# U = v_m w made for four f tiles in one run, and the second matmul's halves reordered at a group's end

## The chip, the cores and the metric

The kernel runs on one core of a Trainium2 chip. The metric is the device time of one execution in microseconds (us). The core has a matrix engine (PE, with its weight loads shown apart as PEld), a vector engine (DVE), a scalar engine (ACT), GpSimd (POOL) and SyncE (SP, which here only issues DMAs).

## The reference, cut to what matters

```python
# batch 8, heads 8, seq 576, head_dim 64, n_mem 32
a   = softmax(phi, axis=seq)
k_m = einsum('bhsm,bhsd->bhmd', a, k);  v_m = einsum('bhsm,bhsd->bhmd', a, v)
attn = softmax(q @ k_m.T / 8, axis=mem)
x   = (attn @ v_m) laid out as (8*576, 512)
gate = sigmoid(x @ w_gate);  val = x @ w_val          # 512 -> 1536
out = (gate * val) @ w_out                            # 1536 -> 512
```

## The kernel before, in words

The kernel never forms x. Since x @ w = attn @ (v_m w), it makes U = v_m w for each batch b and each *f tile* (128 of the 1536 columns of w_gate and the same 128 of w_val, `NFT` = 12 tiles), and multiplies attn by U. Every float32 product is made of three matmuls on halves called hi and lo (hi·hi, hi·lo, lo·hi).

**One step** (b, f) of the main loop (L911) has two halves of the 576 rows, c = 0 (256 rows) and c = 1 (320 rows, of which 64 are put aside in `left` and multiplied later by `out_left`). A half is:
- `gate_of`: 12 matmuls `pu_t<-at_..,u_..` on PE. c = 0 uses one PSUM bank for gate and value, c = 1 uses two. The pool `pu` has `NB` = 4 banks, given out in turn.
- `gate_sig` (ACT, sigmoid, L135), `gate_mul` (DVE, product, L636), `gate_hi` (ACT, cast, L647), `gate_lo` (DVE, difference, L150).
- later `out_half`: 6 matmuls `acc<-wo_..,g_..` with w_out, into the four other PSUM banks (`acc`). Halves wait in the list `pend`; one is taken out whenever it holds `LAG` = 3.

**U** is made for a pair of f tiles (`make_u`, L547). `u_banks` issues 8 matmuls `pu_t<-wg,vT`, one for each head, each on a 64x32 tile of the array and 512 columns wide, into two PSUM banks. `u_hi` (ACT, two casts, L567) and `u_lo` (DVE, two differences, L150) then bring them to SBUF in `u_tiles`, of which the pool keeps two. The heads 4 to 7 read the second half (k = 1) of the weights of an f tile, the heads 0 to 3 the first half (k = 0). The main loop makes the next pair's U in every second step, between its two halves.

**The order of steps.** The steps come in groups of `TURN` = 4 f tiles: for f 0-3 the batches 0 to 3 in turn, then f 4-7 for the same batches, then f 8-11 (these batches are added up through rows that are written to and read back from DRAM, `part`, with `row` as the buffer, `out_end`, L687), and then the batches 4 to 7 with all 12 f tiles each. The first 8 steps are part of a list written out by hand (`OPENING`), which also makes U for the batches 0 and 1 and for (2, f 0-1); the main loop begins with step 8 (`DONE`).

**Work beside it.** The weights come as 64-bit words and are turned into float32 on the way: a job (f, k) is a load on the POOL queue, a magnitude on ACT (L236) and four operations on DVE (L241, L242, L245, L248); k = 0 and 1 are the two halves of w_gate and w_val, k = 2 is w_out, which has a cast (`wo_hi`, L278) and a difference (`wo_lo`) more. `CONVERT` says at which step each job is issued. The attention of the following batch (scores, maximum, exponent, `normalize`, `turn`, and the sums of k and v, `remember`) is spread over the steps in pieces (`sides`); where the next step is another batch's, what is left of the pieces is issued before U is made.

The program order of PE is the order of the Python calls. On ACT and DVE a scheduler orders the work, within chains that keep the gate's sigmoids, products and differences ahead of the weight jobs.

Of the kernel before, what the change touches and what calls it, by code (L numbers as in the profile page):

```python
# [18 lines left out]
B, H, S, D, M = 8, 8, 576, 64, 32  # L19
# [17 lines left out]
TURN = 4  # L37
DONE = 8
# [2 lines left out]

FIRST = 4
CONVERT = {
# [4 lines left out]
}  # L48
# [29 lines left out]
def attn_moe_kernel(  # L78
# [24 lines left out]
    def bank():  # L103
        name = next(turn_of) if spread else None
        if name is None:
            return pu.tile([P, 512], F32, name="pu_t")
        return po.tile([P, 512], F32, name=name)
# [40 lines left out]
    def rest(lo, x, hi):  # L148

        return nc.vector.tensor_tensor(lo, x, hi.bitcast(F32), op=ALU.subtract)  # L150
# [11 lines left out]
    def matmul(*args, **kw):  # L162
        in_turn(nc.tensor.matmul, *args, **kw)
# [145 lines left out]
    def load_q(b, cuts=(0, 1)):  # L309
        if (b, "q") not in loaded:  # L310
            loaded[b, "q"] = att([P, NKT * S], "q")
        for c in cuts:
            for u, n in PIECES[c]:
                o = u * NKT * 2 * P
                move(loaded[b, "q"][:, o : o + NKT * n], qT[b][:, o : o + NKT * n])
# [117 lines left out]
    def of_head(b, w, p):  # L433

        rs = slice((p % 2) * D, (p % 2 + 1) * D)
        hs = slice((p % 4) * M, (p % 4 + 1) * M)
        return rs, kvTs[b][w][rs, p // 4, hs]
# [101 lines left out]
    def again(b):  # L539
        new_at(b)  # L540
        for d, a in zip(kept[b], at[b]):
            move(a.rearrange("p r n -> p (r n)").bitcast(F32), d)
# [1 line left out]

    U = {}

    def make_u(b, fs):  # L547
        u_banks(b, fs)
        u_hi(b, fs)
        u_lo(b, fs)  # L550

    def u_banks(b, fs):

        nf = len(fs)
        pb = [bank()[:, : nf * 256].rearrange("p (f x) -> p f x", f=nf) for _ in range(2)]
        for p in range(H):
            rs, l = of_head(b, 1, p)
            js = slice((p // 2) * M, (p // 2 + 1) * M)
            r = wg[rs, fs[0] : fs[0] + nf, ORDER[b % 2][p] // 2, :]
            matmul(pb[p % 2][js], l, r, start=True, stop=True)  # L560
        loaded[b, "u", fs[0]] = pb

    def u_hi(b, fs):
        pb, nf = loaded[b, "u", fs[0]], len(fs)
        U[b, fs[0]] = u_tiles()
        for r in range(2):
            nc.scalar.copy(U[b, fs[0]][0][:, r, :nf], pb[r])  # L567

    def u_lo(b, fs):
        pb, nf = loaded.pop((b, "u", fs[0])), len(fs)  # L570
        hi, lo = U[b, fs[0]]
        for r in range(2):
            last_u[0] = rest(lo[:, r, :nf], pb[r], hi[:, r, :nf])
        for i, f in enumerate(fs):
            U[b, f] = (hi[:, :, i], lo[:, :, i])
# [22 lines left out]
    def gate_half(b, f, c):  # L598
        gate_of(b, f, c)
        gate_sig(b, f, c)  # L600
        gate_mul(b, f, c)
        gate_hi(b, f, c)
        gate_lo(b, f, c)
# [56 lines left out]
    def out_half(b, f, c, at_start, at_end):  # L660
        out_of(b, f, c, at_start, at_end)
        if at_end:
            out_end(b, f, c)
        if (b, f + 1) in ends and c:
            for t in range(2):
                rows[b, t] = row_of(b, t)

    def out_of(b, f, c, at_start, at_end):
        hi, lo = G.pop((b, f, c))
        w_hi, w_lo = wo_of(f)  # L670
        for j in range(2):
            t = 2 * c + j
            if at_start:
                acc[b, t] = po.tile([P, DM], F32, name=f"acc{t}")
            ts = slice(j * P, (j + 1) * P)
            o = acc[b, t]
            matmul(o, hi[:, ts], w_hi, start=at_start, stop=False)
            matmul(o, hi[:, ts], w_lo, start=False, stop=False)
            matmul(o, lo[:, ts], w_hi, start=False, stop=at_end)

    def out_end(b, f, c, js=range(2)):
        for j in js:
            t = 2 * c + j
            o = acc.pop((b, t))
            st = rows.pop((b, t), None) or row_of(b, t)
            if (b, t) in part:
                nc.vector.tensor_tensor(st, o, st, op=ALU.add)  # L687
                part.pop((b, t))
            elif t % 2:
                nc.scalar.copy(st, o)  # L690
            else:
                nc.vector.tensor_copy(st, o)
            if f == NFT - 1:
                move(out[b * S + t * P : b * S + (t + 1) * P, :], st)
            else:
                part[b, t] = dram.tile([P, DM], F32, name=f"part{b}_{t}_{f}")
                move(part[b, t], st)
# [3 lines left out]
    def row_of(b, t):  # L701

        st = mb.tile([P, DM], F32, name="row", bufs=2)
        if (b, t) in part:
            move(st, part[b, t], "rows")
        return st

    def u_tiles():
        return [mb.tile([P, 2, 2, 256], F32R, name=f"u_{p}", bufs=2) for p in ("hi", "lo")]
# [3 lines left out]
    def out_left(pair, f0, nf):  # L713

        hi, lo = [t.rearrange("p r f x -> p (r f x)").rearrange("p (f x) -> p f x", x=P) for t in u_tiles()]
        for k in range(0, nf, TURN):
            raw = left.pop((pair, (f0 + k) // TURN))
            nc.scalar.copy(hi[:, k : k + TURN], raw)
            rest(lo[:, k : k + TURN], raw, hi[:, k : k + TURN])
        yield  # L720
        o = bank()
        for k in range(nf):
            w_hi, w_lo = wo_of(f0 + k)
            matmul(o, hi[:, k], w_hi, start=(k == 0), stop=False)
            matmul(o, hi[:, k], w_lo, start=False, stop=False)
            matmul(o, lo[:, k], w_hi, start=False, stop=(k == nf - 1))
        if f0 == 0:
            left_sum[pair] = mb.tile([P, DM], F32, name="wo_raw")
            nc.vector.tensor_copy(left_sum[pair], o)
        else:  # L730
            st = left_sum.pop(pair)
            nc.vector.tensor_tensor(st, o, st, op=ALU.add)
            for j in range(2):
                b = 2 * pair + j
                move(out[b * S + SF * P : (b + 1) * S, :], st[j * TAIL : (j + 1) * TAIL, :])
        yield


    def run(*parts):
        for p in parts:  # L740
            for _ in p:
                pass
# [39 lines left out]
    steps = [(b, f, f == f0, f == f1 - 1) for b, f0, f1 in turns for f in range(f0, f1)]  # L782
    ends = {(b, f) for b, f, _, at_end in steps if at_end}
    begin = {(b, f): i for i, (b, f, at_start, _) in enumerate(steps) if at_start}

    u_at = {}
    for i, (b, f, _, _) in enumerate(steps):
        if f % 2 == 0:
            u_at[i - 1] = (b, [f, f + 1])

    spare = ident.bitcast(mybir.dt.bfloat16)
    idle = po.tile([P, 512], F32, name=f"acc{SF - 1}")
# [104 lines left out]
        begin[turns[k - 1][:2]]: b for k, (b, f0, _) in enumerate(turns) if b < QUAD and f0  # L897
    }
    lefts = {begin[2, NFT - TURN]: 0, begin[QUAD, 0]: 1, begin[QUAD + 2, 0]: 2}
    lefts = {i + 2 * k: (p, 8 * k, 8 - 4 * k) for i, p in lefts.items() for k in range(2)}  # L900
    lefts[begin[B - 1, 0] + 8] = (B // 2 - 1, 0, 8)

    beside, slots = iter(()), iter(())

# [5 lines left out]
    pend = [(1, f, c, False, f == 3) for f in (2, 3) for c in range(2)][-LAG:]  # L910
    for i, (b, f, at_start, at_end) in enumerate(steps):  # L911
        if i < DONE:
            continue
        if i in sides:
            run(beside)
            beside, slots = chain(*sides[i][1:]), iter(sides[i][0])
        if i in returns:
            again(returns[i])
        if i > max(CONVERT) and (QUAD, "q") not in loaded:
            load_q(QUAD)  # L920
        extra = out_left(*lefts[i]) if i in lefts else iter(())
        gate_half(b, f, 0)
        for job in CONVERT.get(i, ()):
            with behind():
                convert(*job)
        next(extra, None)
        if i in u_at:
            if steps[i + 1][0] != b:
                run(beside)
            make_u(*u_at[i])  # L930
        while len(pend) >= LAG:
            out_half(*pend.pop(0))
        pend.append((b, f, 0, at_start, at_end))
        go_on()
        gate_half(b, f, 1)
        while len(pend) >= LAG:
            out_half(*pend.pop(0))
        pend.append((b, f, 1, at_start, at_end))
        next(extra, None)
        go_on()  # L940
        del U[b, f]
# [58 lines left out]
```

## Time and profile before

| | |
|---|---|
| median of 3 runs | 763.07 us (761.05 to 764.59) |
| the profiled execution | 762.09 us |
| its span in the profile | 760.3 us |
| PE busy | 737.1 us (97%) |
| DVE busy | 434.6 us (57%) |
| ACT busy | 337.6 us (44%) |
| granted TensorE clock | 0.992 of full speed |

The profiled execution's time is 1.8 us more than its span, which begins and ends with the first and last thing that the profile shows. A row of the timeline gives the start, the duration, the engine, the line, the operation, output<-inputs, shapes and a count; a matmul's duration overlaps the next one's, so the pace of PE is read from start to start. In square brackets stands idle time of the engine ahead of the row and what ended it.

### The profile page before, as it was taken

What the parts mean: (1) busy time and instruction counts of PE and PEld (TensorE: products, weight loads), DVE (VectorE), ACT (ScalarE), POOL (GpSimd) and SP (SyncE); (2) the same over time, 40 slices, a digit from 0 to 9 for tenths busy, and PEclk for the clock granted to TensorE, in tenths of its full rate; (3) what the DMA queues carried; (4) which work ended last, traced back from release to release, by engine and by line L of the source; (5) the groups of instructions that cost most, each with busy time, mean ns of one, the idle gap of its engine ahead of it and who ended that gap; (6) DMA issues with size and microseconds to landing.
All of it is one profiled execution on the core that took longest, in us unless ns stands there. A gap on an engine that the chain in (4) does not pass through costs nothing.

```text
span 760.3 us, 13810 instructions
## 1 busy us (share of the span) xinstructions
PE 737.1 (97%) x5651; PEld 610.0 (80%) x5651; DVE 434.6 (57%) x824; ACT 337.6 (44%) x784; POOL 14.1 (2%) x30
## 2 busy tenths in 40 slices
PE   7998999998999999999999999999999999999997
PEld 5676887786887888888887888887887888888886
DVE  7897748995777754456646533365333743343422
ACT  4387545575443443235442643355333533333322
POOL 0000000011000000000000000000000000000000
PEclk9899999999999999999999999999999999999999
DMA  9977255767555453432462240011000000010002
GB/s 358 363 287 288 84 208 186 263 227 244 213 196 187 170 181 112 159 113 75 132 212 70 91 152 6 1 56 63 2 2 28 28 15 1 1 56 1 1 1 69
DMA packets 30655, 93.17 MB, mean 123 GB/s; under 512 B 3456, under 2 KB 4480, under 8 KB 28032
## 3 DMA queue, kind: packets, MB, share of 16 engines
q1 hardware_dynamic: 22528, 71.31, 25.8%
q0 software_dynamic: 3456, 12.58, 5.0%
q10 hardware_dynamic: 4608, 8.39, 3.5%
q8 instruction: 44, 0.72, 0.4%
q14 instruction: 19, 0.16, 0.1%
HBM read 69.73 MB, written 22.54 MB: 121 GB/s over the span
## 4 chain that ended last, share of the span: by engine, by line
PE 86%; ACT 4%; DVE 4%; DMA 3%; issue 1%; SPq 0%; DVEq 0%; ACTq 0%
PE pu_t L160 51%; PE acc L160 35%; DMA kvm<-in_kvm_dram 2%; ACT L135 2%; ACT ph L135 1%; DMA part<-row 1%; DVE q L513 1%; ACT sg L135 0%; DMA row<-part 0%; DVE u_lo L150 0%; DVE sg L636 0%; DVE e L492 0%; DVE g_lo L150 0%; SPq L146 0%; DVE at_lo L150 0%
## 5 line engine op out<-in xcount | busy, mean ns | idle before, releaser
L160 PE MATMUL pu_t<-at_hi,u_hi 128*128 128x256 f32 (+1 forms) x760 | 227.0, 299 | 0.9 <-DVE sg L636 0.9
L160 PE MATMUL pu_t<-at_hi,u_lo 128*128 128x256 f32 (+1 forms) x760 | 223.0, 293 | 1.1 <-DVE u_lo L150 1.1
L160 PE MATMUL pu_t<-at_lo,u_hi 128*128 128x256 f32 (+1 forms) x760 | 223.4, 294 | 0.0
L636 DVE TENSOR_TENSOR sg<-pu_t,sg 128x256 f32<-128x256 f32 (+1 forms) x190 | 86.4, 455 | 190.0 <-ACT sg L135 117.3
L135 ACT ACTIVATE sg<-pu_t 128x256 f32<-128x256 f32 (+1 forms) x190 | 78.3, 412 | 209.5 <-PE pu_t L160 196.0
L160 PE MATMUL acc<-wo_hi,g_hi 128*128 128x512 f32 x384 | 156.9, 409 | 1.4 <-DVE row L687 1.4
L160 PEld LDWEIGHTS pu_t<-at_hi,u_hi 128*128 128x128 f32 x760 | 142.7, 188 | 12.3 <-DVE sg L636 2.2
L160 PE MATMUL acc<-wo_hi,g_lo 128*128 128x512 f32 x384 | 151.3, 394 | 0.0
L160 PE MATMUL acc<-wo_lo,g_hi 128*128 128x512 f32 x384 | 151.1, 394 | 0.0
L160 PEld LDWEIGHTS pu_t<-at_lo,u_hi 128*128 128x128 f32 x760 | 142.7, 188 | 6.5
L160 PEld LDWEIGHTS pu_t<-at_hi,u_lo 128*128 128x128 f32 x760 | 142.5, 187 | 1.5 <-DVE u_lo L150 1.5
L647 ACT CAST g_hi<-sg 128x256 fp32r<-128x256 f32 x192 | 78.0, 406 | 131.7 <-DVE sg L636 118.3
L150 DVE TENSOR_TENSOR g_lo<-sg,g_hi 128x256 fp32r<-128x256 f32 x192 | 80.6, 421 | 56.0 <-ACT g_hi L647 55.8
L160 PEld LDWEIGHTS acc<-wo_hi,g_hi 128*128 128x128 f32 x384 | 72.2, 188 | 49.7 <-issue 38.5
L160 PEld LDWEIGHTS acc<-wo_hi,g_lo 128*128 128x128 f32 x384 | 72.4, 189 | 17.1
L160 PEld LDWEIGHTS acc<-wo_lo,g_hi 128*128 128x128 f32 x384 | 72.4, 189 | 8.7
L150 DVE TENSOR_TENSOR u_lo<-pu_t,u_hi 128x512 fp32r<-128x512 f32 x93 | 60.6, 684 | 3.8 <-ACT u_hi L567 2.6
L160 PE MATMUL pu_t<-wg,vT 64*32 64x512 f32 x744 | 52.8, 601 | 2.8 <-DVE wg L248 2.8
L567 ACT CAST u_hi<-pu_t 128x512 fp32r<-128x512 f32 x93 | 49.9, 587 | 5.3 <-PE pu_t L160 3.6
L687 DVE TENSOR_TENSOR row<-acc,row 128x512 f32<-128x512 f32 x32 | 21.9, 687 | 8.7 <-DMA row<-part 5.1
L135 ACT ACT_TABLE_LOAD x20 | 25.7, 1283 | 2.1 <-DVE g_lo L150 1.0
L160 PE MATMUL acc<-ident 128*128 128x256 bf16 x155 | 23.0, 313 | 1.4 <-POOL ident masks.py:199 1.4
(110 smaller groups left out, 574.1 us busy)
## 6 DMA issues: line engine op xcount, KB each, us to landing
kvm<-in_kvm_dram SPq DMA_DIRECT2D x16, 1024.0 KB, 8.2
q<-in_qT_dram SPq DMA_DIRECT2D x16, 512.0 KB, 5.3
part<-row SPq DMA_DIRECT2D x32, 256.0 KB, 2.3
row<-part ACTq DMA_DIRECT2D x32, 256.0 KB, 3.1
out_dram<-row SPq DMA_DIRECT2D x32, 256.0 KB, 2.0
words<-in_wgv_dram POOLq DMA_DIRECT2D x10, 512.0 KB, 4.8
ph<-in_phiT_dram SPq DMA_DIRECT2D x8, 576.0 KB, 4.9
at_hi<-at SPq DMA_DIRECT2D x8, 576.0 KB, 3.9
```

Source lines behind the costliest of these rows:

```text
L135: last_act[0] = nc.scalar.activation(*args, **kw)
L150: return nc.vector.tensor_tensor(lo, x, hi.bitcast(F32), op=ALU.subtract)
L160: last_pe[0] = do(*args, **kw)
L513: nc.vector.transpose(t.rearrange("p r n -> p (r n)"), loaded[b, "e"])
L567: nc.scalar.copy(U[b, fs[0]][0][:, r, :nf], pb[r])
L636: last_prod[0] = nc.vector.tensor_tensor(sg, val, sg, op=ALU.mult)
L647: nc.scalar.copy(ghi, prod[:, : 2 * P])
L687: nc.vector.tensor_tensor(st, o, st, op=ALU.add)
```

## The change

U is made for the four f tiles of a group in one run of 16 matmuls: all four PSUM banks are filled first, and then come the casts and differences of the first pair and of the second. It is made at the end of the group before, behind the last half's gate matmuls, instead of in every second step between the halves. Only the pair (2, f 2-3) is still made alone, at step 9. After a run all waiting output halves but one are issued at once, so that two stand behind the run and none between the next group's first three gate halves. The jobs of w_gate and w_val for f 4 to 7 are issued earlier than those of w_out for them, from step 10 instead of 11, and the left rows' pieces (`lefts`) move to the steps 2 and 6 of a batch (10 for the last), where they began at 0 and 2 (8).

```diff
 CONVERT = {
-    11: [(4, 0)], 12: [(4, 1), (4, 2)], 13: [(5, 0), (5, 1)], 14: [(5, 2), (6, 0)], 15: [(6, 1), (6, 2)],
-    16: [(7, 0), (7, 1)], 18: [(7, 2)], 19: [(8, 0)], 20: [(8, 1)], 21: [(8, 2)], 22: [(9, 0)],
+    10: [(4, 0)], 11: [(4, 1)], 12: [(5, 0), (5, 1)], 13: [(6, 0), (6, 1)], 14: [(4, 2), (7, 0)], 15: [(7, 1), (5, 2)],
+    16: [(6, 2)], 18: [(7, 2)], 19: [(8, 0)], 20: [(8, 1)], 21: [(8, 2)], 22: [(9, 0)],
...
-    def make_u(b, fs):
-        u_banks(b, fs)
-        u_hi(b, fs)
-        u_lo(b, fs)
+    def make_u(b, *pairs):
+        for fs in pairs:
+            u_banks(b, fs)
+        for fs in pairs:
+            u_hi(b, fs)
+            u_lo(b, fs)
...
-        if f % 2 == 0:
-            u_at[i - 1] = (b, [f, f + 1])
+        if f % TURN == 0 and i > DONE:
+            u_at[i - 1] = (b, [f, f + 1], [f + 2, f + 3])
...
-    lefts = {i + 2 * k: (p, 8 * k, 8 - 4 * k) for i, p in lefts.items() for k in range(2)}
-    lefts[begin[B - 1, 0] + 8] = (B // 2 - 1, 0, 8)
+    lefts = {i + 2 + 4 * k: (p, 8 * k, 8 - 4 * k) for i, p in lefts.items() for k in range(2)}
+    lefts[begin[B - 1, 0] + 10] = (B // 2 - 1, 0, 8)
...
-        if i in u_at:
-            if steps[i + 1][0] != b:
-                run(beside)
-            make_u(*u_at[i])
+        if i == DONE + 1:
+            make_u(b, [2, 3])
...
         pend.append((b, f, 1, at_start, at_end))
+        if i in u_at:
+            if steps[i + 1][0] != b:
+                run(beside)
+            make_u(*u_at[i])
+            while len(pend) > 1:
+                out_half(*pend.pop(0))
```

How this moves PE's instructions, in the last batch (`pu_t<-wg,vT` is U, `pu_t<-at_..` a gate, `acc<-wo_..` an output half). Before, U stands behind the first half's gate:

```order
L160 MATMUL pu_t<-at_hi,u_hi 128x256
L160 MATMUL pu_t<-at_lo,u_hi 128x256
L160 MATMUL pu_t<-at_hi,u_lo 128x256
L160 MATMUL pu_t<-wg,vT 32x512 x8
L160 MATMUL acc_7501<-wo_hi,g_hi 128x512
L160 MATMUL acc_7501<-wo_lo,g_hi 128x512
L160 MATMUL acc_7501<-wo_hi,g_lo 128x512
```

Now the run of 16 stands between output halves, at the end of the group:

```order
L160 MATMUL acc_7477<-wo_hi,g_hi 128x512
L160 MATMUL acc_7477<-wo_lo,g_hi 128x512
L160 MATMUL acc_7477<-wo_hi,g_lo 128x512
L160 MATMUL pu_t<-wg,vT 32x512 x16
L160 MATMUL acc_7501<-wo_hi,g_hi 128x512
L160 MATMUL acc_7501<-wo_lo,g_hi 128x512
L160 MATMUL acc_7501<-wo_hi,g_lo 128x512
```

There are 21 such runs of 16; 42 runs of 8 have gone.

On DVE, the end of the job (7, 1), whose result the heads 4 to 7 of U for f 6-7 read. Before it is done in step 16 to 17, ahead of every `u_lo` of those tiles:

```order
L245 SCALAR_TENSOR_TENSOR wg<-words,wg 128x512
L150 TENSOR_TENSOR g_lo<-sg,g_hi 128x256
L248 SCALAR_TENSOR_TENSOR wg<-words,wg 128x512
L150 TENSOR_TENSOR u_lo<-pu_t,u_hi 128x512
L692 COPY row<-acc_1922 128x512
L150 TENSOR_TENSOR u_lo<-pu_t,u_hi 128x512
```

Now it is due at the end of step 15, and its last operation (L248) stands behind the first difference of the same run of U:

```order
L245 SCALAR_TENSOR_TENSOR wg<-words,wg 128x512
L150 TENSOR_TENSOR u_lo<-pu_t,u_hi 128x512
L248 SCALAR_TENSOR_TENSOR wg<-words,wg 128x512
L241 TENSOR_SCALAR wo_raw<-wo_raw 128x512
L150 TENSOR_TENSOR u_lo<-pu_t,u_hi 128x512
L242 TENSOR_SCALAR wo_raw<-wo_raw 128x512
L150 TENSOR_TENSOR u_lo<-pu_t,u_hi 128x512
```

## The prediction

> **What bounds the kernel now.** I read the page first (busy shares and the chain that ended last), then PE's waits, then the timeline around a run of U.
>
> ```profile
> PE 737.1 (97%) x5651; PEld 610.0 (80%) x5651; DVE 434.6 (57%) x824; ACT 337.6 (44%) x784; POOL 14.1 (2%) x30
> PE 86%; ACT 4%; DVE 4%; DMA 3%; issue 1%; SPq 0%; DVEq 0%; ACTq 0%
> PE pu_t L160 <- DVE wg L248: 2.8, 1, 2.8
> PE pu_t L160 <- DVE u_lo L150: 1.4, 3, 0.9
> PE acc L160 <- DVE row L687: 1.4, 1, 1.4
> ```
>
> PE is the bound: 86% of the chain. The three lines are the largest of its waits after the opening (total, times, longest), few and single. So the change is worth what it takes out of PE's stream, plus or minus such waits. What a step costs PE is seen from start to start, here steps 10 and 11:
>
> ```profile
> 122.04 0.28 PE L160 MATMUL pu_t<-at_hi,u_hi 128*128 128x256 f32 x1
> 123.45 0.40 PE L160 MATMUL acc<-wo_hi,g_hi 128*128 128x512 f32 x1
> 124.84 0.31 PE L160 MATMUL pu_t<-at_hi,u_hi 128*128 128x320 f32 x1
> 126.60 0.39 PE L160 MATMUL acc<-wo_hi,g_hi 128*128 128x512 f32 x1
> 127.98 0.28 PE L160 MATMUL pu_t<-at_hi,u_hi 128*128 128x256 f32 x1
> ```
>
> The first half's gate takes 1.41 us, the second's 1.76, an output half 1.38 (0.23 a matmul).
>
> **A run of U.** Its 8 matmuls show as 16 records, two passes.
>
> ```profile
> 218.38 0.28 PE L160 MATMUL pu_t<-at_lo,u_hi 128*128 128x256 f32 x1
> 218.50 0.28 PE L160 MATMUL pu_t<-at_hi,u_lo 128*128 128x256 f32 x1
> 218.71 1.09 PE L160 MATMUL pu_t<-wg,vT 64*32 64x512 f32 x16
> 219.73 0.50 PE L160 MATMUL acc<-wo_hi,g_hi 128*128 128x512 f32 x1
> 220.07 0.40 PE L160 MATMUL acc<-wo_lo,g_hi 128*128 128x512 f32 x1
> L160 PE MATMUL pu_t<-wg,vT x744: 589/589/614, 29.6 to 731.2; 64*32 64x512 f32 x186
> ```
>
> The gate matmul at 218.50 would be followed 0.12 later, at 218.62; the output matmul at 219.73 takes 0.34 to the next start instead of 0.23. The run so costs 220.07 - 0.23 - 218.62 = 1.22 us, and the last row says that all runs are alike (589 to 614 ns). What a second group of 8 costs in the same run, no U shows. The nearest rows are the scores, also 8 tiles of 64x32: once 16 records of 256 columns alone, once with a further 16 of 64 columns in the run (x32).
>
> ```profile
> 333.72 0.40 PE L160 MATMUL acc<-wo_hi,g_lo 128*128 128x512 f32 x1
> 334.05 0.66 PE L160 MATMUL pu_t<-q,kT 64*32 64x256 f32 x16
> 334.64 0.42 PE L160 MATMUL pu_t<-at_hi,u_hi 128*128 128x320 f32 x1
> 334.90 0.31 PE L160 MATMUL pu_t<-at_lo,u_hi 128*128 128x320 f32 x1
> 343.19 0.40 PE L160 MATMUL pu_t<-wo_hi,u_lo 128*128 128x512 f32 x1
> 343.51 0.78 PE L160 MATMUL pu_t<-q,kT 64*32 64x256 f32 x32
> 344.22 0.39 PE L160 MATMUL pu_t<-at_hi,u_hi 128*128 128x256 f32 x1
> 344.45 0.28 PE L160 MATMUL pu_t<-at_lo,u_hi 128*128 128x256 f32 x1
> ```
>
> Counted in the same way, the first costs 334.75 - 333.95 = 0.80 and the second 344.33 - 343.42 = 0.91: 0.11 for 64 columns, and no new entry or exit. At eight times the columns a second group of U is 0.88, against 1.22 for a run of its own: 0.34 saved, in 21 runs 7.1 us. The ends: nothing saved, if two groups of 512 columns don't follow each other as the scores do, and 0.36 (7.6 us), if part of the 0.11 is fixed. I take 7.1, since the scores are the same tiles on the same engine.
>
> [...]
>
> **What covers the moved work.** Behind a run there are two output halves, 2 x 1.38 = 2.76 us, before the next group's first gate needs the first pair's U.
>
> ```profile
> L567 ACT CAST u_hi<-pu_t 128x512 fp32r<-128x512 f32 x93 | 49.9, 587 | 5.3 <-PE pu_t L160 3.6
> L150 DVE TENSOR_TENSOR u_lo<-pu_t,u_hi 128x512 fp32r<-128x512 f32 x93 | 60.6, 684 | 3.8 <-ACT u_hi L567 2.6
> L687 DVE TENSOR_TENSOR row<-acc,row 128x512 f32<-128x512 f32 x32 | 21.9, 687 | 8.7 <-DMA row<-part 5.1
> 92.00:184.00 92.00, 86.56 (x670) 70.33 (x669) 68.84 (x133) 52.18 (x118) 7.47 (x13) 1.00 0.63 220
> 340.00:760.00 420.00, 414.39 (x3021) 345.30 (x3019) 192.84 (x364) 166.95 (x399) 0.00 (x0) 1.00 0.15 49
> ```
>
> The first pair is in PSUM some 0.9 us before the run's end. Two casts and the second difference (0.59 + 0.59 + 0.68, with 0.3 for the hand-overs) end 1.3 us after the run's end: 1.5 us to spare. The second pair's four operations end 2.6 us after it, and are wanted two steps later. All four banks hold U then; the gates of the next group need them one after the other from 2.8 us on, so they are free. Without output halves between them, three gate halves (4.58 us) follow each other, and ACT and DVE must turn them over. The windows (span, then busy PE, PEld, DVE, ACT) give DVE 75% from 92 to 184 and 46% after 340, ACT 57% and 40%. I cost this at 0 after step 16. In the groups with row sums, the two sums of the first rows (0.69 each) now stand on DVE behind the four differences and ahead of the next product. They can begin when the output half before them ends and end about 4.1 us after the run's end (2.76 less half an output half, 0.3, two sums), while that product's gate ends at 4.5 (2.76 + 1.41 + 0.3): hidden too, if the old rows have landed.
>
> **Waits that are there now, one by one.**
>
> ```profile
> 135.25 0.39 PE L160 MATMUL pu_t<-at_hi,u_hi 128*128 128x256 f32 x1
> 137.67 0.39 PE L160 MATMUL pu_t<-at_hi,u_lo 128*128 128x256 f32 x1 [0.92 <-DVE u_lo L150]
> 138.60 0.39 PE L160 MATMUL acc<-wo_hi,g_hi 128*128 128x512 f32 x1
> 172.02 1.06 PE L160 MATMUL pu_t<-wg,vT 64*32 64x512 f32 x8
> 175.89 1.06 PE L160 MATMUL pu_t<-wg,vT 64*32 64x512 f32 x8 [2.81 <-DVE wg L248]
> 176.88 0.50 PE L160 MATMUL acc<-wo_hi,g_hi 128*128 128x512 f32 x1
> 241.19 0.50 PE L160 MATMUL acc<-wo_hi,g_hi 128*128 128x512 f32 x1 [1.42 <-DVE row L687]
> 432.29 0.41 PE L160 MATMUL pu_t<-at_hi,u_hi 128*128 128x320 f32 x1 [0.71 <-DVE sg L636]
> 517.66 0.41 PE L160 MATMUL pu_t<-at_hi,u_hi 128*128 128x320 f32 x1 [0.16 <-DVE sg L636]
> ```
>
> And two rows of DVE, the ends of the jobs (5, 0) and (7, 0):
>
> ```profile
> 150.56 0.68 DVE L248 SCALAR_TENSOR_TENSOR wg<-words,wg 128x512 int32<-128x512 int32 x1
> 170.04 0.68 DVE L248 SCALAR_TENSOR_TENSOR wg<-words,wg 128x512 int32<-128x512 int32 x1
> ```
>
> - Step 12's first gate waits for `u_lo` of step 11: from 135.25 to 138.60 it takes 3.36 us instead of 1.41, so 1.95 are lost. Now the differences have 2.76 us of cover. But the run's second pair needs the banks of the half just before it, whose product stands on DVE behind the attention's transposes; I put it at about 135.6, with the run's start at 133.9 (127.98 + 1.41 + 1.38 + 1.76 + 1.38) and the second pair due at 134.9. That is 0.7 of wait (0 to 1.95): gain 1.25. The run then ends at 136.7, and the next gate begins at 139.5.
> - The run for (0, f 6-7) in step 17 takes 176.88 - 172.02 = 4.86 us instead of 1.02: 3.84 lost to the job (7, 1). Now that job is due at the end of step 15. From the end of step 11's four differences (140.8, my estimate: DVE has the attention until about 138.4, and they take 2.4) seven jobs remain up to (7, 1). Six took 19.5 us before (150.56 to 170.04), with one pair of differences among them; so about 7 x 3.25 - 1.2 = 21.5 us, to 162.3. PE comes to the run at 139.5 + 4 x (1.41 + 1.76) + 6 x 1.38, near 160.5. But L248 stands behind the first difference of this very run: pair one 0.95, hand-over 0.25, cast 0.59, difference 0.68, L248 0.68 and 0.05, so 3.2 us from the start at the least, where the heads 4 to 7 would otherwise go on at 1.0 and share the array with the others. The second half then takes 1.0: at least 4.2 instead of 1.9, a wait of 2.3, and about 2.6 with DVE a little late (up to 4.8, below). Gain 1.25 (1.5 to -1).
> - At 239 an output half waits for the row sums, which go through two buffers and DRAM (1.42, and 0.3 for the restart). Between the sums and the next use of these banks there are now three gates without output, some 1.9 us more: gain 1.7 (0 to 1.9).
> - At 432 and 517 the second gate half of a step waits because the attention's long DVE operations and `u_lo` of the pair made in that step stand ahead of the product that frees its bank: 0.71 and 0.16, and some 0.27 each for the restart. There is no U there any more: gain 1.4 (0 to 1.4).
>
> The matmuls, casts and differences are the same in number, and so are the tail and the opening to step 10: 0. Weight loads of w_out for f 5 to 7 come up to two steps later and are first used at the end of step 18: 0. The `lefts` only move.
>
> **Sum:** 7.1 + 1.25 + 1.25 + 1.7 + 1.4 = 12.7 us, from the profiled execution's 762.1: 749.4. The median of the runs is 1.0 higher, so 750.4; I say 750.5. A change within 0.5% (3.8 us) can hardly be told from none here.
>
> **Rivals.**
> - *Two groups cost as much as two runs*: the array empties between the pairs, or the second pair waits for its banks each time. For it: 512 columns were never seen in one run. Against it: the scores. Only the waits are gained: 762.1 - 5.6 + 1.0 = 757.5. Chance 0.10.
> - *The weights for f 6-7 come later still*: with 3.8 us a job instead of 3.25, (7, 1) ends at 166.2 and the run at 167.2 instead of 162.4: 4.8 lost instead of 3.84, and step 12 keeps its wait. For it: DVE has 75% of work in this stretch, and it serves gates and attention first. 762.1 - 7.1 + 1.0 - 1.7 - 1.4 + 1.0 = 753.9. Chance 0.17.
> - *Slower*: the beginning of every group waits for DVE. Place: the next group's first gate on `u_lo` of the first pair, behind 1.5 us of slack. If the chain is x later, 21 groups lose x - 1.5 each; it turns the sign at 12.7 / 21 = 0.6 (x = 2.1) and makes the kernel measurably slower at x = 2.3. With x = 2.6 it is 749.4 + 23 + 1.0 = 773.5. Against it: nothing long stands between the last product and the first difference in most groups, and DVE is idle half the time. Chance 0.05.
> - *More than forecast*: step 11's run doesn't wait, step 15's waits only 2.3, and each term is at its good end: 762.1 - 7.6 - 1.95 - 1.5 - 1.9 - 1.4 + 1.0 = 748.7. Chance 0.08.
>
> My forecast has 0.60 (748 to 753). The range of 747 to 756 leaves out the slower rival and nearly all of the first. Faster by more than 0.5%: 0.91; within: 0.04; slower: 0.05.
>
> **What would show it.** Runs of U with 32 records that cost PE 2.1 us (1.22 + 0.88), not 2.4; gates after them without a wait on `u_lo`; one run near 160 cut in two, with PE waiting 2 to 3 us for L248; no waits near 240, 430 and 517. I am wrong if the 32 records show a gap in the middle, or if waits of 0.5 us and more stand at most group starts.

## The result, and the profile after

| | before | changed |
|---|---|---|
| median of the runs, us | 762.06 (759.38 to 764.59, 4 runs) | 754.33 (753.58 to 754.74, 4 runs) |
| profiled execution, us (its span) | 762.1 (760.3) | 754.74 (753.0) |

The ratio is 0.9903, with a 95% interval of 0.9877 to 0.993: faster by 7.7 us of the 12.7 that the sum had promised; 754.33 us stands where the forecast was 750.5. The page of the changed kernel and its largest waits of PE after the first 92 us (total, times, longest):

```profile
PE 729.6 (97%) x5651; PEld 609.9 (81%) x5651; DVE 432.4 (57%) x824; ACT 337.7 (45%) x784; POOL 13.7 (2%) x30
PE 87%; DMA 5%; DVE 4%; ACT 2%; issue 1%; SPq 1%; ACTq 0%; DVEq 0%
PE pu_t L160 <- DVE wg L248: 2.3, 2, 1.8
PE pu_t L160 <- ACT ph L135: 1.8, 1, 1.8
PE pu_t L160 <- ACT sg L135: 1.4, 2, 1.1
PE pu_t L160 <- DVE sg L638: 0.4, 1, 0.4
```

PE's busy time fell by 7.5 us (737.1 to 729.6). From step 10 on the waits on `u_lo` and on the row sums are gone (0.3 for `u_lo` and 0.7 for L393 remain ahead of step 10, as before). The one on the weights (L248) is still there, a wait on the sigmoid `sg` is new, and the one on `ph` has grown. Before, the last of these was:

```profile
PE pu_t L160 <- ACT ph L135: 0.5, 1, 0.5
```

Where the 7.35 us between the two profiled executions lie is seen if each is cut at the first gate of step 10. These are that gate and the last matmul, in the changed kernel:

```profile
123.79 0.28 PE L160 MATMUL pu_t<-at_hi,u_hi 128*128 128x256 f32 x1
747.56 0.39 PE L160 MATMUL pu_t<-wo_hi,u_lo 128*128 128x512 f32 x1
```

From one to the other it takes 623.77 us; before, from 122.04 to 754.88, it took 632.84. So 9.07 us were gained where the change is, and 1.75 lost ahead of it, in the opening.

A run of U, rows as in the prediction:

```profile
326.49 0.40 PE L160 MATMUL acc<-wo_hi,g_lo 128*128 128x512 f32 x1
326.81 1.95 PE L160 MATMUL pu_t<-wg,vT 64*32 64x512 f32 x32
328.69 0.50 PE L160 MATMUL acc<-wo_hi,g_hi 128*128 128x512 f32 x1
329.03 0.40 PE L160 MATMUL acc<-wo_lo,g_hi 128*128 128x512 f32 x1
L160 PE MATMUL pu_t<-wg,vT 64*32 64x512 f32 x744 | 49.3, 596 | 3.1 <-DVE wg L248 2.3 <-DVE sg L638 0.4 <-ACT sg L135 0.3
```

The 32 records stand in one row, with no gap in the middle. An output matmul would have followed at 326.72; the run costs 329.03 - 0.23 - 326.72 = 2.08 us, where two runs cost 2 x 1.22. The last row (all of U; busy, mean ns; idle time before it, by releaser) says that only 3.1 us of waiting stand in the runs. All of it is in two places; of the 21 runs 18 take 1.87 or 1.88 us from their start to the next matmul, the other three are those of step 11 (2.35) and of the two places. The first is step 15 and what follows it (DVE's and ACT's rows are by time among PE's):

```profile
162.09 1.09 PE L160 MATMUL pu_t<-wg,vT 64*32 64x512 f32 x16
163.71 1.06 PE L160 MATMUL pu_t<-wg,vT 64*32 64x512 f32 x8 [0.53 <-DVE wg L248]
165.22 0.68 DVE L150 TENSOR_TENSOR u_lo<-pu_t,u_hi 128x512 fp32r<-128x512 f32 x1
165.82 0.68 DVE L248 SCALAR_TENSOR_TENSOR wg<-words,wg 128x512 int32<-128x512 int32 x1
166.55 1.06 PE L160 MATMUL pu_t<-wg,vT 64*32 64x512 f32 x8 [1.78 <-DVE wg L248]
167.55 0.50 PE L160 MATMUL acc<-wo_hi,g_hi 128*128 128x512 f32 x1
173.35 1.28 ACT L135 ACT_TABLE_LOAD   x1
174.65 0.78 ACT L135 ACTIVATE ph<-ph,nmx 128x576 f32<-128x576 f32 x1
175.57 0.66 PE L160 MATMUL pu_t<-ident,ph 128*128 128x128 f32 x4 [1.83 <-ACT ph L135]
```

The run goes from 162.09 to 167.55, 5.46 us instead of 1.88: 3.58 lost (3.05 in the second profile of the changed kernel, where the first of the two waits is missing). Its last weights, job (7, 1), end at 166.50 on DVE, behind the first difference of the same run. The first of the two waits (0.53) is named for L248 in the row, but the operation that ended before it is the product that frees a bank, on DVE until 162.97. Then, at the end of step 16, PE waits for the exponentials of `phi` for b 4: in that step its two gate halves now follow each other with no output half between them, and it is there before ACT has loaded its table. That loses 1.99 us, 0.67 before.

The second place is the end of the fourth step of b 5 (step 63):

```profile
512.24 1.15 ACT L523 CAST at_hi<-q 128x1152 fp32r<-128x1152 f32 x1 [2.05 <-DVE q L513]
512.69 1.09 PE L160 MATMUL pu_t<-wg,vT 64*32 64x512 f32 x16
513.43 1.36 DVE L150 TENSOR_TENSOR at_lo<-q,at_hi 128x1152 fp32r<-128x1152 f32 x1 [0.91 <-ACT at_hi L523]
513.61 0.43 ACT L135 ACTIVATE sg<-pu_t 128x320 f32<-128x320 f32 x1
514.09 1.04 PE L160 MATMUL pu_t<-wg,vT 64*32 64x512 f32 x2 [0.31 <-ACT sg L135]
515.04 0.48 DVE L638 TENSOR_TENSOR sg<-pu_t,sg 128x320 f32<-128x320 f32 x1
515.58 1.09 PE L160 MATMUL pu_t<-wg,vT 64*32 64x512 f32 x14 [0.45 <-DVE sg L638]
```

The run's second pair needs the banks of the gate half just before it. They come free with that half's sigmoid and product, and ahead of these stand the attention's casts for b 6, `at_hi` on ACT and `at_lo` on DVE. From 512.69 to the output half at 516.59 it takes 3.90 us instead of 1.88: 2.02 lost. The run in the same place was late before, too. It stands in one row, without a wait beside it, but it took 1.66 us to the next matmul where 40 of the other 41 runs took 1.01 or 1.02; so 0.64 of the loss is old:

```profile
513.30 1.73 PE L160 MATMUL pu_t<-wg,vT 64*32 64x512 f32 x16
514.96 0.51 PE L160 MATMUL acc<-wo_hi,g_hi 128*128 128x512 f32 x1
```

In b 4 and b 6, where 24 matmuls of the left rows (5.5 us of PE) stand just ahead of that step, the same casts are done in time and the run doesn't wait.

A third loss stands outside the runs, at the end of step 40 (ACTq is ACT's issuing of transfers):

```profile
336.59 0.33 ACTq L146 DMA_DIRECT2D row<-part  x1
337.02 0.44 ACT L135 ACTIVATE sg<-pu_t 128x320 f32<-128x320 f32 x1 [2.04 <-DMA out_dram<-row]
337.51 0.39 PE L160 MATMUL pu_t<-at_hi,u_hi 128*128 128x256 f32 x1 [1.09 <-ACT sg L135]
```

Here PE meets the third gate half in a row behind a run of U and waits for the sigmoid that frees its bank. ACT is idle for 2.04 us ahead of that sigmoid; its issue of the load `row<-part` comes first, and by the trace both came free with the end of a transfer `out_dram<-row`. From the scores at 335.64 to this gate it takes 1.87 us, where the same pair took 0.71 before (343.51 to 344.22): 1.16 lost. The second profile has this wait as well (1.01). No experiment here moves that load alone, so its part in the loss is read from the rows, not tested.

### The profile page after: what moved, and what is told of

Its sections match the earlier page's. It is cut to its first block, busy times and chain, and to the rows that moved or that the text cites. A ratio compares the mean times of both kernels' runs of the same rounds, so it can differ in the third digit from the quotient of the medians.

```text
span 753.0 us, 13818 instructions
## 1 busy us (share of the span) xinstructions
PE 729.6 (97%) x5651; PEld 609.9 (81%) x5651; DVE 432.4 (57%) x824; ACT 337.7 (45%) x784; POOL 13.7 (2%) x30
## 4 chain that ended last, share of the span: by engine, by line
PE 87%; DMA 5%; DVE 4%; ACT 2%; issue 1%; SPq 1%; ACTq 0%; DVEq 0%
PE pu_t L160 52%; PE acc L160 36%; DMA kvm<-in_kvm_dram 2%; DMA q<-in_qT_dram 2%; DMA words<-in_wgv_dram 1%; SPq L146 1%; DMA out_dram<-row 1%; ACT L135 1%; ACT ph L135 0%; ACT sg L135 0%; DVE u_lo L150 0%; ACT at_hi L523 0%; DVE g_lo L150 0%; DVE wg L248 0%; DVE at_lo L150 0%
## 5 line engine op out<-in xcount | busy, mean ns | idle before, releaser
L160 PE MATMUL acc<-wo_hi,g_hi 128*128 128x512 f32 x384 | 154.7, 403 | 0.0
L150 DVE TENSOR_TENSOR u_lo<-pu_t,u_hi 128x512 fp32r<-128x512 f32 x93 | 58.3, 683 | 24.7 <-ACT u_hi L569 24.6
L569 ACT CAST u_hi<-pu_t 128x512 fp32r<-128x512 f32 x93 | 48.1, 598 | 27.1 <-PE pu_t L160 27.0
L160 PE MATMUL pu_t<-wg,vT 64*32 64x512 f32 x744 | 49.3, 596 | 3.1 <-DVE wg L248 2.3
L160 PEld LDWEIGHTS pu_t<-wg,vT 64*32 64x32 f32 x744 | 11.4, 105 | 26.0 <-issue 16.6
```

Source lines behind the costliest of these rows:

```text
L160: last_pe[0] = do(*args, **kw)
```

## The experiments

The medians of the experiments come from chips on which the kernel before was timed beside them, with medians of 760.5 to 760.9, so ratios are compared, not times. The two columns in the middle are from each profile: the first gate of step 10, and from there to the last matmul. The last one is how long the granted clock was at 0.5 after PE's wait for `q` near 75 us in the opening, and later (two-microsecond windows, (1 - clock) / 0.5 of each).

| kernel | ratio to before (95%) | step 10 at, us | from there, us | at half clock, us |
|---|---|---|---|---|
| before, first and second profile | 1 | 122.04, 122.06 | 632.84, 633.05 | 3.4 and 0; 6.8 and 3.4 |
| changed, first and second profile | 0.9903 (0.9877 to 0.993) | 123.79, 122.12 | 623.77, 623.19 | 6.8 and 0; 3.4 and 0 |
| e1: runs split | 0.9954 (0.9937 to 0.997) | 122.19 | 628.34 | 6.8; 3.4 |
| e2: weights earlier | 0.9884 (0.986 to 0.9908) | 121.16 | 622.53 | 3.4; 3.4 |
| e3: before with the table | 0.9993 (0.9978 to 1.0007) | 122.00 | 632.04 | 3.4; 6.8 |
| e4: no output halves behind | 1.0137 (1.0112 to 1.0161) | 121.53 | 642.03 | 3.4; 3.4 |
| e5: casts behind the run | 0.9871 (0.9847 to 0.9896) | 123.27 | 621.59 | 6.8; 0 |
| e6: transposes half a step later | 0.9902 (0.9879 to 0.9925) | 122.29 | 623.06 | 6.8; 0 |
| e7: the three edits | 0.9837 (0.981 to 0.9864) | 121.82 | 620.49 | 6.8; 3.4 |
| e8: one output half behind | 0.9919 (0.989 to 0.9948) | 123.49 | 625.94 | 6.8; 3.4 |
| e9: three edits, exponentials one step later | 0.9812 (0.9788 to 0.9835) | 122.44 | 617.74 | 3.4; 0 |
| e10: two steps later | 0.9856 (0.9832 to 0.988) | 121.45 | 621.76 | 3.4; 0 |

**e1, the runs split.** The changed kernel, but

```diff
-            make_u(*u_at[i])
-            while len(pend) > 1:
-                out_half(*pend.pop(0))
+            for fs in u_at[i][1:]:
+                make_u(u_at[i][0], fs)
+                out_half(*pend.pop(0))
```

> The changed kernel, but with one output half between the two pairs of each group: 21 runs of 32 records become 42 of 16, nothing else moves. Theory A (a run has a fixed price of entry and exit, about 0.36 us by the trace of the changed kernel: 2 x 1.22 - 2.08): 21 x 0.36 = 7.5 us more on PE, less what the second pairs no longer wait for their banks (0.46 in step 11, 0.7 in step 15, up to 2.0 near 513 us), so 759 to 762 us; single runs show a cost of 1.2 us each. Rival (merging gained nothing, and all of the gain is the waits): 752 to 755 us.

Two runs of it, with the output half between them:

```profile
133.85 0.40 PE L160 MATMUL acc<-wo_hi,g_lo 128*128 128x512 f32 x1
134.18 1.09 PE L160 MATMUL pu_t<-wg,vT 64*32 64x512 f32 x16
135.19 0.50 PE L160 MATMUL acc<-wo_hi,g_hi 128*128 128x512 f32 x1
135.53 0.40 PE L160 MATMUL acc<-wo_lo,g_hi 128*128 128x512 f32 x1
136.78 1.09 PE L160 MATMUL pu_t<-wg,vT 64*32 64x512 f32 x16
```

Each costs 135.53 - 0.23 - 134.08 = 1.22 us again, and from step 10 on the kernel is 4.57 us slower than the changed one (ratio 0.9954; the 756.6 us of its median lie below the 759 to 762 expected, on a chip where before too was 1.4 us faster). That is the 7.5 of theory A, less what PE no longer loses (0.5 in step 11, 2.1 in step 15, 1.7 in step 63, and 1.2 in step 40, where the wait for the sigmoid is gone too), plus some 1.6 for a clock at 0.5 after the wait in step 16, told below, and some 0.9 in small pieces elsewhere. The rival, that merging gives nothing, is out. It also shows the other side: a merged run asks for four banks and both pairs' weights at once, and 4.3 us of the 7.5 that it saves are paid back in the three places where one of these is late.

**e2, the last weights earlier.** The changed kernel, but

```diff
-    ... 14: [(4, 2), (7, 0)], 15: [(7, 1), (5, 2)],
+    ... 14: [(7, 0), (7, 1)], 15: [(4, 2), (5, 2)],
```

> The changed kernel with the jobs (7, 0) and (7, 1) both ahead of (4, 2): the last weights that step 15's run needs are converted one job (about 3.3 us) earlier and ahead of the run's differences. Theory A (the run's 3.6 us of wait are the job's place on DVE and little else): the wait on the weights goes, about 0.7 for the bank stays, and 2 to 3 us are gained: 751.5 to 752.5 us. Rival (PE only arrives earlier at the next thing that ACT and DVE owe it, the exponentials of step 16, where 2.0 us are lost already): the wait moves there and the time stays at 753.5 to 755 us.

Step 15 takes 2.75 us less: the run goes on for the weights without a stop and loses 0.8, to the bank. But PE waits for the exponentials as before (1.83), and this time the granted clock falls after it (windows of 2 us; busy PE, PEld, DVE, ACT, POOL; clock; DMA):

```profile
168.00:170.00 2.00, 0.36 (x3) 0.10 (x1) 1.70 (x4) 1.99 (x3) 0.15 (x1) 1.00 0.98 301
170.00:172.00 2.00, 1.80 (x10) 1.81 (x11) 1.09 (x4) 2.00 (x8) 1.90 (x4) 0.64 0.95 343
172.00:174.00 2.00, 2.00 (x10) 1.90 (x10) 0.78 (x2) 1.97 (x5) 0.04 (x1) 0.51 1.02 322
```

Step 17 is 1.55 longer for that, and 1.24 are left. Theory A had the mechanism and its size; neither theory had the clock.

**e3, the table alone.** The kernel before, with the new `CONVERT` and nothing else.

> The kernel before with the new table of conversions alone; runs of 8 and output halves stay as they were. Theory A (the table alone removes the wait of step 17, 3.84 us, since (7, 1) then ends some 10 us before that run): 3 to 4 us less than before, 758 to 759.5 us. Rival (the jobs moved ahead of the attention's operations on DVE make steps 11 to 15 wait for as much): within 1 us of before.

The rival holds: 0.9993. Step 17 is 3.53 us shorter, its wait is gone; but the jobs now stand on DVE ahead of the attention's last operations, and step 12's first gate waits for these, and then runs at half the clock (0.50 from 139 to 144 us):

```profile
135.80 0.38 PE L160 MATMUL pu_t<-at_hi,u_hi 128*128 128x256 f32 x1 [0.52 <-ACT at_hi L523]
138.38 0.58 PE L160 MATMUL pu_t<-at_lo,u_hi 128*128 128x256 f32 x1 [2.20 <-DVE at_lo L150]
```

Steps 11 and 12 are 4.0 us longer. In the changed kernel this wait doesn't show; there a run of 2.1 us and a second output half stand ahead of that gate, which may be why. So the parts of the change are not a sum; the table pays only with the rest.

**e4 and e8, less cover.** The changed kernel without the loop behind `make_u` (e4), and with `while len(pend) > 2` instead of `> 1`, so one output half instead of two (e8).

> The changed kernel without the two output halves that were put behind a group's run: the next group's first gate half follows the run at once. In the trace of the changed kernel near 428 us the first pair's second difference ends 1.7 us before the gate begins, behind two halves of 1.38 each. Theory A (slack is what the halves cover): each of 21 starts loses 2.76 - 1.7 = 1.1, and 0.3 for the restart: 28 to 31 us more, 782 to 785 us. Rival (the casts and differences come forward when nothing is ahead of them on ACT and DVE, or PE loses nothing): under 10 us more.

> The changed kernel with one output half behind each group's run instead of two. Without any, a start lost 0.67 us to the differences, so one half of 1.38 leaves 0.7 to spare. Theory A (the starts wait nothing; the second output half stands between the two gate halves of the next step and covers most of the 2.0 us that step 16 loses to the exponentials): 622 to 623 us from the first gate of step 10 to the last matmul instead of 623.8. Rival (two halves are needed, since the row sums or the second pair come late): 626 us or more.

Without cover a start of a group loses 0.67 us, where theory A had 1.4: the first gate needs only the first of the pair's differences to begin (near 197 us that one ends at 197.24, and the gate begins at 197.31). So two halves leave 2.76 - 0.67 = 2.1 us to spare. PE's waits in e4:

```profile
PE pu_t L160 <- DVE u_lo L150: 15.7, 23, 2.3
PE acc L160 <- DVE row L689: 4.0, 2, 3.1
```

These two lines are more than the 18.3 us that e4 is slower from step 10 on; the wait for the row sums comes back too. In e8 nearly all starts go without a wait, as theory A had it, and its gain in step 16 is there: the wait for `ph` is 0.50 us there instead of 1.83, and the wait of step 40 is gone. But step 12's gate waits 0.74 for `u_lo`, the run of step 15 comes earlier and waits longer (two waits of 1.3), with the clock at 0.5 there, and in step 18 an output half waits 0.99 for a copy on ACT that frees its bank (L692). In all e8 is 2.2 us behind the changed kernel, near the rival's 626.

**e5, the casts behind the run.** The changed kernel, but

```diff
-        turn(b)
+        with behind() if b == 6 else ExitStack():
+            turn(b)
...
-        sides[begin[b, 0]] = ([1] * 23, score(b + 1, then), attend(b + 1))
+        sides[begin[b, 0]] = ([1] * 6 + [int(b != 5)] + [1] * 17, score(b + 1, then), attend(b + 1))
```

> The changed kernel with the attention's last operations for b 6 (the transposition and the casts to at_hi and at_lo, in the middle of the fourth step of b 5) put behind that group's run of U. Theory A (the run near 513 us waits 2.0 us because these operations stand on ACT and DVE ahead of the sigmoid and the product that free its banks): that run takes 2.2 us from start to start instead of 4.2, and from the first gate of step 10 to the last matmul it is 621.8 us instead of 623.8. Rival (they now delay the products of the next two gate halves instead): 623 to 625, with the wait near 520 us.

Theory A: 621.59 us (2.4 less in step 63 and 0.4 more in the steps behind it), and the run is whole again:

```profile
512.01 1.95 PE L160 MATMUL pu_t<-wg,vT 64*32 64x512 f32 x32
```

So the order of ACT and DVE, not the banks' number by itself, made the wait of step 63.

**e6, e7, e9 and e10, the exponentials.** In the changed kernel the pieces of `remember(4)` go to the slots `[2, 2, 1, 1, 1, 1, 1]` from step 16 on. e6 has `[2, 1, 2, 1, 1, 1, 1]`, which puts the first transposes half a step later; e7 is e2, e5 and e6 in one; e9 is e7 with `[2, 0, 0, 1, ...]`, e10 with `[2, 0, 0, 0, 0, 1, ...]`.

> The changed kernel with the first transposes of phi for b 4 half a step later (step 17 instead of the end of step 16). Theory A (PE waits 2.0 us in step 16 for the exponentials only because its two gate halves now follow each other with no output half between them): the wait goes, and nothing takes its place: 621.8 us from the first gate of step 10 to the last matmul instead of 623.8. Rival (the exponentials and the table load also hold up the sigmoids, so that PE waits for a bank instead): 623 to 625.

> The changed kernel with three edits at once: the jobs (7, 0) and (7, 1) ahead of (4, 2), the attention's last operations for b 6 behind the run, and the transposes of phi half a step later. Theory A (the three waits are independent, 2.75 + 2.0 + 2.0 us, and without the wait in step 16 the clock does not fall to 0.5 there as it did with the jobs moved alone, 1.6 us): 617 us from the first gate of step 10 to the last matmul, and 0.981 to 0.983 of before. Rival (each hides the next one): 620 to 622 and 0.986 to 0.988.

> The three edits at once, but with the exponentials of phi for b 4 one step later (end of step 17) and their transposes in the middle of step 18, where three output halves are pending again. Theory A (the table loads and exponentials hold ACT for about 4.5 us, and PE gets over that only where output halves are pending; in steps 16 and 17 there is but one): the waits of steps 16 and 17 go (2.4 and 4.2 us of the three edits at once), some 1 us may stay: 615 to 617 us from the first gate of step 10 to the last matmul, 0.975 to 0.98 of before. Rival (ACT's 4.5 us cost PE the same wherever they stand): 619 to 621.

> As the run beside it, but with the exponentials another step later (end of step 18) and the transposes in the middle of step 19, which ends in a group's run of U. Theory A: the same 615 to 617 us from the first gate of step 10 to the last matmul, or up to 2 us more if the copies of phi stand ahead of that run's casts. Rival: 619 to 621.

In e6 step 16 is 2.4 us shorter and step 17 2.2 longer: the rival. Between them the table load, two exponentials and the load back to the sigmoid hold ACT for 4.5 us (by the rows of before, 1.28 for each load and 0.78 and 0.19 for each exponential), and PE then waits for a bank whose sigmoid stands behind them. In e7 the same happens, at half the clock (0.50 from 176 to 178 us), and eats 4.2 us of the three gains, so that its 620.49 us is the rival's time (its ratio, 0.9837, lies between the two theories'):

```profile
175.41 0.42 PE L160 MATMUL pu_t<-at_hi,u_hi 128*128 128x320 f32 x1 [1.97 <-ACT e L359]
```

e9 moves the exponentials to where three output halves are pending again. Its waits of PE after the first 92 us:

```profile
PE pu_t L160 <- ACT e L393: 1.3, 2, 0.7
PE pu_t L160 <- ACT sg L135: 1.0, 1, 1.0
```

One of the two for L393 stands ahead of step 10, as in every run; the one for `sg` is that of step 40. 617.74 us is 6.0 less than the changed kernel, 0.7 over theory A's range; its median is 747.07 us, 0.9812 of before (expected 0.975 to 0.98), and it is the fastest of all. Against the changed kernel: step 15 -2.8, step 63 -2.4, and steps 16 to 19 together -1.1. These four are not to be compared one by one: work of PE moved with the exponentials (-2.9 in steps 16 and 17, +1.8 in steps 18 and 19), and at the end of step 19 PE waits 0.66 for the keys' copies (L393) ahead of a run. e10, another step later, is 6.1 longer in steps 18 and 19, where PE waits for the copies of phi (2.0 for L351) and for `ph` (1.0): more than expected, and the rival's time. ACT is idle for 4.25 us just ahead of the exponentials there (0.00 busy from 178 to 180 us); pending output halves alone don't make a place good.

**The two kernels once more**, for a second profile of each.

> The changed kernel once more, unchanged, for a second profile. Theory A (the first gate of step 10 came at 123.8 us in the first profile and at 122.0 in that of before only because the clock was at 0.5 for longer after the wait in the opening, and this changes from one execution to the next): it comes at 121 to 123 this time, and from there to the last matmul it is 623.8 us within 0.3 (or up to 1.7 more, if the clock falls after the wait in step 16). Rival (the change itself makes the opening longer): 123.5 or more again.

> The kernel before once more, unchanged. Theory A: 632.8 us within 0.3 from the first gate of step 10 to the last matmul (or up to 1.7 more, if the clock falls after the wait in step 17); the first gate of step 10 anywhere between 121 and 124 us. Rival: 122.0 us again within 0.2.

The changed kernel's step 10 came at 122.12 us instead of 123.79 (752.51 us in all), before's at 122.06, which fits both its theory and its rival. So the 1.75 us lost in the opening were the execution's, not the change's. In the first and the second profile of the changed kernel PE waits 4.2 us for the load of `q`, begins again at 76.17 and at 75.62, and meanwhile the clock falls (windows of 2 us):

```profile
74.00:76.00 2.00, 0.00 (x0) 0.00 (x0) 0.00 (x0) 1.49 (x6) 0.00 (x0) 0.81 0.28 115
76.00:78.00 2.00, 1.83 (x18) 0.95 (x19) 0.65 (x2) 0.00 (x0) 0.00 (x0) 0.50 0.00 0
78.00:80.00 2.00, 2.00 (x6) 1.12 (x4) 1.97 (x7) 0.26 (x1) 0.00 (x0) 0.50 0.00 0
80.00:82.00 2.00, 2.00 (x36) 1.36 (x36) 0.88 (x3) 0.77 (x2) 0.53 (x1) 0.50 0.00 0
```

```profile
76.00:78.00 2.00, 2.00 (x19) 1.49 (x5) 1.64 (x7) 0.00 (x0) 0.00 (x0) 0.54 0.00 0
78.00:80.00 2.00, 2.00 (x36) 0.87 (x35) 1.34 (x2) 1.00 (x2) 0.09 (x1) 0.61 0.00 0
```

In the first, the clock is at 0.5 for 6.8 us, in the second for 3.4. The fourteen profiles tell what that costs: from PE's restart to step 10 it is 46.4 to 46.6 us in the seven with 3.4 us at half clock and 47.5 to 47.9 in the seven with 6.8, and the restart comes between 74.15 and 76.17 us. So theory A of the first of these runs had the larger part, not all. Against before's first profile (restart at 75.51) the changed kernel's had 0.66 of the 1.75 us from the later restart and 1.1 from the clock; before's second profile had 6.8 us too, but an early restart, at 74.29. Later before's second profile had 3.4 us of half clock after the wait of 0.91 in step 12, where its first had none, and that step took 9.45 us instead of 7.87; the wait for the row sums near 239 was 1.1 us shorter, so that the whole from step 10 on is the same within 0.2.

## Why the prediction was right, and where it wasn't

754.33 us lies inside the range of 747 to 756, but outside the 748 to 753 of the forecast itself. Four terms put at 0 lost 5.7 us between them. The range held because it had room for other rivals, not because these losses were foreseen; that is in part luck. Term by term, from the first profile of each kernel (gain in us, a minus for a loss):

| term | predicted | measured |
|---|---|---|
| one run instead of two, 21 times | 7.1 | 7.5 |
| step 12's first gate | 1.25 | 1.5 |
| weights for f 6-7 | 1.25 | 0.3 |
| transposes of phi in step 16 | 0 | -1.3 |
| output half near 239, row sums | 1.7 | 1.7 |
| gate halves near 432 and 517 | 1.4 | 1.4 |
| run of step 63 (2.0 lost now, 0.6 before) | 0 | -1.4 |
| gate at the end of step 40 | 0 | -1.2 |
| pieces of less than 0.3, not traced | 0 | 0.6 |
| opening | 0 | -1.75 |
| sum | 12.7 | 7.35 |

- **The main term was right**, and for the reason given. A second group in the same tiles pays no new entry and exit (2.08 us for a run of 16, 1.22 for one of 8 alone); the row of the scores was the right one to take, and e1, which takes the merging back, loses it again. One reading beside it was wrong: the row with 589 to 614 ns says that the matmuls are alike, not that the runs are, and the run of step 63 was 0.64 us late already.
- **Step 12** was right in kind: the second pair of step 11's run does wait for a bank, 0.46 us where 0.7 was put.
- **The weights of step 15** were mis-sized: 3.58 us lost (3.05 in the second profile), where "about 2.6" was said. Job (7, 1) ended at 166.50, not at 162.3. The 3.25 us a job came from a stretch in which only one pair of differences stood between the jobs; the rival with 3.8 us a job had 166.2. That L248 would stand behind the first difference of its own run was right, as the rows of step 15 show, and e2 takes the wait away by moving one job.
- **"I cost this at 0 after step 16"** is the step that failed, three times. The sum asked whether ACT and DVE turn over three gate halves in a row; it answered from their average load and looked at the gates alone. What PE met there were pieces of other work that had been placed for the old rhythm: the exponentials of step 16 (1.99 us lost instead of 0.67), the attention's casts in step 63 (2.02 instead of 0.64), and in step 40 a sigmoid behind a load that ACT issues (1.16). For the casts the prediction had the mechanism at hand (it used it for step 11: the second pair needs the bank of the half just before it, whose product stands on DVE behind the attention) and, in the same step of b 5, removed a 0.43 wait that these operations made. It didn't ask where the casts would be late next. e5 shows that they are the cause; e9 against e7 shows it for the exponentials (2.9 us less in steps 16 to 19). Step 40 stays untested.
- **The cover behind a run** is larger than the 1.5 us of the prediction: 2.1 us by e4. The "slower" rival was far away. For the row sums behind it the prediction's own terms add up to 3.75 us (2.76 less 0.69, 0.3 and 2 x 0.69), not to 4.1; either is less than 4.5, so nothing hangs on it.
- **The row sums near 239**: gone as predicted, but of the 1.7 us about 1.1 belonged to that execution of before. In its second profile the wait was 0.3, not 1.42; that this term came out to the tenth is luck.
- **Opening and executions**: at 0 the prediction was right for the change, and blind to what one execution can differ from the next by: 121.2 to 123.8 us at step 10 over fourteen profiles. From step 10 on the two profiles of each kernel differ by 9.1 to 9.9 us; the medians, over all runs, by 7.7, with an interval of some 5.3 to 9.4 (0.993 and 0.9877 of 762). Whether the opening makes up the difference, the profiles don't show.

The two rivals that gave about the measured time (757.5, and 753.9 with the weights late) were not the cause: the merging was worth its full price, and the late weights were about a quarter of what was missing from step 10 on (1.0 of 3.6 us).

## What to carry to other kernels

When work is merged into bigger runs, list what each bigger run needs at once (banks, weights, converted halves), and at each place where it will stand look up who frees these and what is queued ahead of that on its engine; the average slack says nothing about the one place where a long operation is in the way. When output work is moved out from between two pieces, everything placed by hand in that gap has lost its cover too, and must be placed anew: here that was worth two thirds of the change itself (6.0 us beside 9.1). And a change in a table that removes a wait may earn nothing alone: take the time from one fixed point of the program to another, and see who waits next.

## What was not expected of the hardware

The granted clock of TensorE falls to 0.5 after some waits of PE, for 3.4 or 6.8 us in each of the 21 cases that fourteen profiles show from 70 us on. A spell of 3.4 us costs up to 1.6 us more than the wait itself (step 17 in e2: 7.99 us instead of 6.44; step 12 in before's second profile: 9.45 instead of 7.87). It is not fixed by the wait's length: 1.83 us in step 16 brought it in e1 and e2 and not in the changed kernel's two profiles, 0.91 us in step 12 brought it in one profile of before and not in the other, and 2.8 us in step 17 brought it in neither.

In the first profile of before the clock falls at 17.45 and 75.48 us and is back at 24.28 and 78.89; in that of the changed kernel it falls at 17.21 and 75.23 and is back at 24.04 and 82.06. Within each of the two profiles these times lie whole multiples of 3.413 us apart, to 0.01. In windows of that length, counted from each profile's own changes, what PE did can be read. In the 3.41 us ahead of each of the seven later falls it was busy for 1.1 to 1.6 us in six (e2 from 167.13 to 170.54: 1.58) and for 2.29 in the seventh (before's second profile, from 135.11). The clock stayed at 1.0 over the wait in step 16 of the changed kernel's two profiles, with 2.06 and 1.81 us busy in the emptiest window, and over the 2.8 us of before, with 2.03 and 1.99; but it also stayed with 1.52 us (e10, from 190.72) and 1.63 (the changed kernel, from 163.98). So no clean limit comes out of this.
